# A Conformer block on one core: the list scheduler takes in the head and the first loads, and models the copies as one line

## Chip, cores and metric

The kernel runs on 1 core of one Trainium2 chip. The metric is the device time in microseconds; before the change it is 1916.58 us, the median of 3 runs (1914.57 to 1916.84). The core's engines are named as in the profile: PE (TensorE; PEld are its weight loads), DVE (VectorE), ACT (ScalarE), POOL (GpSimd) and SP (SyncE, which issues nearly all copies). A "copy" below is a DMA transfer.

## The reference

One Conformer block on x of shape 2 x 4000 x 512 in bf16 (B = 2, T = 4000, D = 512, F = 2048, a convolution over 3 tokens):

```python
h = _layernorm(x);  h = _silu(h @ w_ff1_a) @ w_ff1_b
x1 = x + 0.5 * h
h = _layernorm(x1); q, k, v = h @ w_q, h @ w_k, h @ w_v
p = _softmax(einsum('btd,bsd->bts', q, k) * scale)
x2 = x1 + einsum('bts,bsd->btd', p, v) @ w_o
h = _layernorm(x2) @ w_pw1;  h = h[..., :D] * _sigmoid(h[..., D:])
dc = depthwise convolution of h over 3 tokens with dw
dc = (dc - mean over all tokens) / sqrt(variance over all tokens + 1e-05)
x3 = x2 + _silu(dc) @ w_pw2
h = _layernorm(x3); h = _silu(h @ w_ff2_a) @ w_ff2_b
return _layernorm(x3 + 0.5 * h)
```

## The kernel before

**Tiles and stages.** The 8000 tokens are cut into 16 chunks of 4 tiles of 127 tokens (the last chunk of each batch is shorter). The program (`program`, L2515) goes through four stages:

1. The head: x of chunk 0 and the first feed-forward's weights are loaded, chunk 0 is normalised and transposed on TensorE, and its first four blocks are computed (`head`, L1131). It takes the first 12 us.
2. First feed-forward (`ff1`, L2566), chunk by chunk, to about 410 us. Beside it the next chunk's x is loaded (`load_x`, L1013), normalised (`ln_job`, L1064) and transposed by a copy (`transpose`, L980: 128 KB, one for each tile); x1 goes out to a DRAM buffer (`put_x`, xd) and the normalised tokens to another (keysd).
3. Attention, to about 1412 us, one group of queries after the other. Keys are read back from keysd, transposed by copies (`key_queries`, L2178) and combined on VectorE into a form stored in DRAM (kfd); values go the same way (v12d). The groups of attention load both again, 384 KB and 256 KB at a time. The convolution of finished chunks runs beside it; its output is stored (dcvd).
4. From 1412 us: the last convolution, the statistics over all tokens, and the second feed-forward (`ff2`, L2798), with x from xd and the convolution from dcvd (`fetch_conv`, L2365), which ScalarE turns into SiLU values (`swish`, L2433).

A second version of the program, for scores beyond a limit, stands behind a branch and does not run with these inputs.

**What sets the order of the work.** Every instruction is emitted through `Sync`, which adds the semaphore waits that its reads and writes need. Each engine executes its own list in order: an instruction that waits holds up all that stand behind it on that engine. Up to L2539 (loads, constants, head) the order is the order of the program. From `S.planned(16000, 8000)` at L2541 on, instructions are collected as nodes of a `Plan` and emitted at the end in the order that a list scheduler finds (`Plan.run`, L234).

The scheduler runs a model of the five engines six times (`once`, L256) and keeps the order with the earliest end. A node has a duration `dur` on its engine, and a time `land` after its start when its result can be read. Each node also has a due time `late`. For TensorE's nodes it is their start in the pass before; for the others it is counted backwards from the readers (L261). An engine takes, of the nodes that are ready in the model, the one that is due first, unless this would hold up one that is ready soon and due earlier (`choose`, L272). A node may be taken up to 16000 ns of TensorE work ahead of TensorE's oldest open node (L283); TensorE itself may swap work within 8000 ns.

A copy's cost before (`Plan.dma`, L213) depends on its own size alone, in ns and bytes:

```python
dur = 1000 + size / 400 if turn else 450 * len(calls)
land = dur + 2600 if turn else dur + 2000 + size / 200
```

`turn` marks a transposing copy. Copies do not slow each other down in this model. The loads ahead of L2541 are not in the plan at all: for the plan their data is there from the start.

Instructions emitted by the plan all carry line L93 in the profile (the recorded call), so they are told apart by the tiles they write and read: wff are the feed-forward weights and stage buffers in the same place, xt the x tiles and, during attention, the loaded keys and values, keys the hidden activations, keys and convolution data, work the small buffers with normalised tokens, sums the matmul operands made on VectorE, s and y the PSUM banks.

Of the kernel before, what the change touches and what calls it, by code (L numbers as in the profile page):

```python
# [61 lines left out]
class Ev:  # L62
    __slots__ = ("key", "val", "snap")
# [7 lines left out]
class Buf:  # L71
# [3 lines left out]
    __slots__ = ("name", "w", "r", "excl", "alias")  # L75
# [9 lines left out]
class Call:  # L85

    __slots__ = ("name", "args", "kw")
# [16 lines left out]

class Node:

    __slots__ = ("e", "emit", "dur", "land", "preds", "succs", "left", "ready", "late", "at", "seq", "ev")


class Plan:  # L110

    PASSES = 6
    TABLES = {AF.Silu: 1, AF.Exp: 2, AF.Tanh: 2, AF.Sigmoid: 3, AF.Sqrt: 4}
    AFTER = {"PE": 65, "ACT": 45, "DVE": 45, "POOL": 60, "SP": 60}
    OVER = {"PE": 0, "ACT": -100, "DVE": -84, "POOL": -60, "SP": 42}
# [56 lines left out]
    def new(self, e, dur, land, emit, reads, writes, dkeys=()):  # L172
        n = Node()
        n.e, n.dur, n.land, n.emit, n.preds, n.succs, n.seq, n.at = e, dur, land, emit, set(), [], len(self.nodes), len(self.pe)
        self.nodes.append(n)
        n.preds |= self.link(n, reads, writes, dkeys)
        return n

    def op(self, e, fn, reads, writes, inc):
# [3 lines left out]
        if e != "PE":  # L183
            n = self.new(e, dur, dur, [lambda: S.emit_op(e, call, reads, writes, inc)], reads, writes)
            if e == "ACT" and call.name == "activation":
                self.tables(n, self.TABLES.get(call.given("func", 2)))
            return
# [25 lines left out]
    def dma(self, engs, dkey, fns, reads, writes):  # L213
        calls = [fn(Probe()) for fn in fns]
        S = self.S
        size = sum(c.given("out", 0).nbytes() if callable(c.given("out", 0).nbytes) else c.given("out", 0).nbytes for c in calls)
        turn = "transpose" in calls[0].name
        dur = 1000 + size / 400 if turn else 450 * len(calls)
        land = dur + 2600 if turn else dur + 2000 + size / 200
        assert len(set(engs)) == 1  # L220
        n = self.new(engs[0], dur, land, [], reads, writes, (dkey,))

        def emit():
            n.ev = S.emit_dma(engs, dkey, calls, reads, writes)

        n.emit.append(emit)
        return n

    def lag(self, a, b):
# [4 lines left out]
    def run(self):  # L234
# [10 lines left out]
        best = None  # L245
        for _ in range(self.PASSES):
            end, order, starts = self.once()
# [8 lines left out]
    def once(self):  # L256

        pe, T = self.pe, self.T
        for n in reversed(self.nodes):
            if n.e != "PE":  # L260
                n.late = min([s.late - self.lag(n, s) for s in n.succs] + [pe[min(n.at, len(pe) - 1)].late + 40000])  # L261
        free = {e: 0.0 for e in self.AFTER}
        wait = {e: [] for e in self.AFTER}
        for n in self.nodes:
            n.left, n.ready = len(n.preds), 0.0
            if not n.left:
                wait[n.e].append(n)
        head, done, starts = 0, [False] * len(pe), [0.0] * len(pe)
        index = {n: k for k, n in enumerate(pe)}
        order = []  # L270

        def choose(e):  # L272
            if e == "PE":
                best = None
                for n in wait["PE"]:
                    k = index[n]
                    if T[k] - T[head] > self.beside:
                        continue
                    key = (max(free[e], n.ready - (40 if k == head else 0)), k)
                    if best is None or key < best[0]:  # L280
                        best = (key, n)
                return best and (max(free[e], best[1].ready), best[1])
            limit = T[head] + self.ahead  # L283
            found = [n for n in wait[e] if T[n.at] <= limit]
            if not found:
                return None
            now = max(free[e], min(n.ready for n in found))
            can = sorted([n for n in found if n.ready <= now], key=lambda n: (n.late, n.seq))
            soon = [n for n in found if n.ready > now]
            for n in can:  # L290
                end = now + n.dur + self.OVER[e]
                if all(end <= u.ready + 60 or u.late >= end or u.late >= n.late for u in soon):
                    return now, n
            u = min(soon, key=lambda n: n.ready)
            return max(free[e], u.ready), u

        ask = dict.fromkeys(free, True)
        said = {}
        while len(order) < len(self.nodes):
            for e in free:  # L300
                if ask[e]:
                    said[e], ask[e] = choose(e), False
            s, n = min([c for c in said.values() if c], key=lambda c: c[0])
            wait[n.e].remove(n)
            ask[n.e] = True
            free[n.e] = s + n.dur + self.OVER[n.e]
            order.append(n)
            if n.e == "PE":
                k = index[n]
                done[k], starts[k] = True, s  # L310
                if k == head:
                    while head < len(pe) and done[head]:
                        head += 1
                    ask = dict.fromkeys(free, True)
            for u in n.succs:
                lag = self.lag(n, u)
                u.ready = max(u.ready, s if lag is None else s + lag)
                u.left -= 1
                if not u.left:
                    wait[u.e].append(u)  # L320
                    ask[u.e] = True
        return free["PE"], order, starts
# [197 lines left out]
class Conformer:  # L520
# [1994 lines left out]
    def program(self, any_score):  # L2515
        i = self.i
        self.any_score = any_score
        S = self.S
        self.reset_schedule()
        self.out_evs = []  # L2520
        self.ring, self.third, self.fourth = list(range(4)), None, None
        self.place(0, self.slot(0, 5))

# [13 lines left out]

        self.act(self.nr1, self.onef, AF.Silu, [self.b_onef], [self.b_nr1])
        self.head()  # L2539
        if not any_score:  # L2540
            S.planned(16000, 8000)  # L2541

        def weights():
            for n, name in (("q", "w_q"), ("k", "w_k"), ("v", "w_v")):
# [352 lines left out]
```

## Time and profile before

| | |
|---|---|
| median of 3 runs | 1916.58 us |
| the profiled execution | 1912.87 us, with a span of 1909.0 us from first to last instruction |
| mean granted clock of TensorE | 0.995 |
| copies | 231.82 MB, 121 GB/s over the span |
| SyncE's queue | 45.8% of the 16 copy engines' span; ScalarE's queue 0.1% |

The rows that the steps below use of copies, from their issue to their landing (the middle value of each group):

| copy | number, size | us to landing |
|---|---|---|
| work<-work, transposing | 206 | 2.5 |
| keys<-keysd, transposing | 62 | 3.4 |
| xt<-kfd | 98 of 384 KB | 3.2 |
| xt<-v12d | 105 of 256 KB | 2.9 |
| kfd<-xt (store) | 14 of 384 KB | 3.8 |
| keys<-dcvd | 12 of 508 KB | 4.3 |
| wff<-in_w_ff_a_dram | 15 of 256 KB | 5.4 |
| wff<-in_w_ff_b_dram | 8 of 512 KB | 7.3 |

How to read it. In the timeline a line gives the start, the length, the engine, the instruction and its tiles as out<-in, and in brackets how long the engine had been idle before it and what ended that. Merged instructions of one kind share a line, with their number behind an x. The releaser in brackets is inferred: a wait for several semaphores is put down to the one that came last. TensorE's busy time counts from a matmul's start to its modelled end, at whatever clock was granted.

### The profile page before, as it was taken

What the parts mean: (1) busy time and instruction counts of PE and PEld (TensorE: products, weight loads), DVE (VectorE), ACT (ScalarE), POOL (GpSimd) and SP (SyncE); (2) the same over time, 40 slices, a digit from 0 to 9 for tenths busy, and PEclk for the clock granted to TensorE, in tenths of its full rate; (3) what the DMA queues carried; (4) which work ended last, traced back from release to release, by engine and by line L of the source; (5) the groups of instructions that cost most, each with busy time, mean ns of one, the idle gap of its engine ahead of it and who ended that gap; (6) DMA issues with size and microseconds to landing.
All of it is one profiled execution on the core that took longest, in us unless ns stands there. A gap on an engine that the chain in (4) does not pass through costs nothing.

```text
span 1909.0 us, 38976 instructions
## 1 busy us (share of the span) xinstructions
PE 1869.8 (98%) x15359; PEld 1505.4 (79%) x15362; DVE 1574.6 (82%) x3315; ACT 1178.3 (62%) x2061; POOL 132.5 (7%) x235
## 2 busy tenths in 40 slices
PE   8999999999999999999999999999988999999998
PEld 5899999965777777777577777777764899999897
DVE  6789888858788889888888788878976888888875
ACT  4777777644555555566346555655556777777773
POOL 1000000000000000000000000000011000000000
PEclk9999999999999999999999999999999999999999
DMA  7333344297655565457944553454366222312211
GB/s 188 83 84 87 84 113 105 58 273 194 168 139 142 153 184 159 116 130 173 239 125 124 134 124 109 128 139 118 112 192 171 61 61 77 77 46 59 51 42 33
DMA packets 333645, 231.82 MB, mean 121 GB/s; under 512 B 208264, under 2 KB 305867, under 8 KB 333199
## 3 DMA queue, kind: packets, MB, share of 16 engines
q1 hardware_dynamic: 332777, 228.91, 45.8%
q8 instruction: 123, 2.02, 0.4%
q14 instruction: 67, 0.55, 0.1%
q10 hardware_dynamic: 678, 0.34, 0.1%
HBM read 128.30 MB, written 55.65 MB: 96 GB/s over the span
## 4 chain that ended last, share of the span: by engine, by line
PE 90%; DVE 4%; DMA 3%; SPq 2%; issue 1%; ACT 1%; DVEq 0%
PE y L93 46%; PE s L93 44%; SPq L93 2%; DVE work L93 1%; DVE sums L93 1%; DVE s L93 1%; DVE wff L93 1%; DVE xt L93 1%; DMA keys<-dcvd 0%; DMA kfd<-xt 0%; SPq L978 0%; DMA wff<-in_w_ff_b_dram 0%; DMA keys<-keysd 0%; DMA wff<-keysd 0%; DMA work<-work 0%
## 5 line engine op out<-in xcount | busy, mean ns | idle before, releaser
L93 ACT ACTIVATE sums<-s 128x508 bf16<-128x508 f32 (+2 forms) x494 | 289.1, 585 | 281.9 <-PE s L93 281.1
L93 ACT ACTIVATE keys<-s 128x508 bf16<-128x508 f32 (+1 forms) x281 | 163.8, 586 | 189.7 <-PE s L93 165.6
L93 PE MATMUL y<-work,keys 128*127 128x256 bf16 x1920 | 244.7, 273 | 0.0
L93 PE MATMUL s<-work,keys 128*128 128x254 bf16 (+5 forms) x1456 | 228.5, 293 | 2.6 <-DVE xt L93 2.4
L93 DVE TENSOR_TENSOR sums<-sums 128x508 bf16<-128x508 bf16 (+4 forms) x528 | 193.7, 398 | 40.9 <-ACT sums L93 37.5
L93 PEld LDWEIGHTS y<-work,keys 128*127 128x127 bf16 x1920 | 216.3, 137 | 5.2
L93 PE MATMUL y<-wff,keys 128*127 128x256 bf16 (+3 forms) x1592 | 209.2, 276 | 0.1
L93 DVE BATCH_NORM_STATS2 work<-xt 127x6 f32<-127x512 bf16 x307 | 201.7, 681 | 5.9 <-DMA xt<-in_x_dram 4.7
L93 PE MATMUL y<-sums,keys 128*128 128x254 bf16 (+1 forms) x1440 | 202.5, 270 | 0.0
L93 PE MATMUL s<-sums 128*128 128x254 bf16 x1296 | 194.3, 273 | 0.0
L93 DVE TENSOR_TENSOR keys<-keys 128x1016 bf16<-128x1016 bf16 (+2 forms) x262 | 168.1, 660 | 31.0 <-ACT keys L93 23.5
L93 PEld LDWEIGHTS y<-wff,keys 128*127 128x127 bf16 (+1 forms) x1592 | 176.1, 136 | 14.1 <-issue 3.3
L93 PE MATMUL y<-work,wff 128*128 128x254 bf16 (+2 forms) x1116 | 184.0, 292 | 0.0
L93 ACT ACTIVATE work<-xt,work 127x512 bf16<-127x512 bf16 x204 | 162.1, 810 | 12.6 <-DVE work L93 12.6
L93 POOL TENSOR_TENSOR work<-work 127x4 f32<-127x4 f32 (+3 forms) x90 | 89.9, 1000 | 1124.9 <-DVE work L93 1124.7
L93 PEld LDWEIGHTS y<-sums,keys 128*128 128x128 bf16 x1440 | 139.1, 97 | 26.4 <-issue 0.6
L93 PEld LDWEIGHTS s<-work,keys 128*128 128x128 bf16 (+1 forms) x1456 | 119.2, 97 | 51.0 <-issue 3.3
L93 DVE TENSOR_TENSOR work<-work,sums 128x508 f32<-128x508 f32 (+1 forms) x224 | 150.5, 672 | 2.5
L93 PE MATMUL s<-work,wff 128*128 128x508 bf16 (+3 forms) x596 | 138.6, 366 | 5.4 <-ACT keys L93 3.4
L93 PE MATMUL y<-sums,xt 128*128 128x254 bf16 (+1 forms) x960 | 142.4, 270 | 0.3 <-DVE sums L93 0.2
L93 PEld LDWEIGHTS s<-sums 128*128 128x128 bf16 x1296 | 126.7, 98 | 18.1
L93 PE MATMUL s<-work 128*127 128x512 bf16 (+3 forms) x528 | 130.8, 377 | 0.6 <-ACT work L93 0.6
(156 smaller groups left out, 3168.7 us busy)
## 6 DMA issues: line engine op xcount, KB each, us to landing
xt<-kfd SPq DMA_DIRECT2D x98, 384.0 KB, 3.2
xt<-v12d SPq DMA_DIRECT2D x105, 256.0 KB, 2.9
xd<-xt SPq DMA_DIRECT2D x28, 448.0 KB, 2.9
xt<-xd SPq DMA_DIRECT2D x28, 448.0 KB, 4.1
out_dram<-xt SPq DMA_DIRECT2D x14, 448.0 KB, 3.2
dcvd<-wff SPq DMA_DIRECT2D x48, 127.0 KB, 2.1
keys<-dcvd SPq DMA_DIRECT2D x12, 508.0 KB, 4.3
xt<-in_x_dram SPq DMA_DIRECT2D x13, 448.0 KB, 4.1
```

The source lines that it names most:

```text
L93: return getattr(eng, self.name)(*self.args, **self.kw)
```

## The change

The plan starts earlier: `S.planned(16000, 8000)` moves from behind the head to the start of the program, ahead of the first loads. The loads of x and of the first feed-forward's weights, the constants' memsets and the whole head become nodes of the plan. Two of these loads carry issuers of both SyncE and ScalarE; the assertion that a copy has one issuer is dropped, and such a node stands on its first issuer, SyncE.

Copies get a size and pass through one line in the model. A copy begins to move when it is issued and the line is free, moves at 260 bytes a ns (180 for a transposing one), and can be read 1000 ns after its last byte. So a copy behind others lands later in the model. The closed formulas for `dur` and `land` change too; they serve where the line's answer of a pass is not there yet. `choose` counts a copy as taking at least its time on the line. And a copy's due time is 3000 ns earlier than its readers ask (`SPARE`).

```diff
 class Plan:
+    SPARE = 3000
...
-        dur = 1000 + size / 400 if turn else 450 * len(calls)
-        land = dur + 2600 if turn else dur + 2000 + size / 200
-        assert len(set(engs)) == 1
+        dur = 800 + size / 350 if turn else 450 * len(calls)
+        land = 1600 + size / 180 if turn else dur + 1400 + size / 260
...
+        n.size, n.turn = size, turn
...
-                n.late = min([s.late - self.lag(n, s) for s in n.succs] + [pe[min(n.at, len(pe) - 1)].late + 40000])
+                n.late = min([s.late - self.lag(n, s) - (self.SPARE if n.size else 0) for s in n.succs] + [pe[min(n.at, len(pe) - 1)].late + 40000])
...
-        order = []
+        order, pipe = [], 0.0
...
-                end = now + n.dur + self.OVER[e]
+                end = now + max(n.dur, n.size / 260) + self.OVER[e]
...
             order.append(n)
+            if n.size:
+                begin = max(s + (400 if n.turn else n.dur + 400), pipe)
+                pipe = begin + n.size / (180 if n.turn else 260)
+                n.land = pipe - s + 1000
...
     def program(self, any_score):
...
+        if not any_score:
+            S.planned(16000, 8000)
...
         self.head()
-        if not any_score:
-            S.planned(16000, 8000)
```

No instruction's operands, tile or amount of work changes; the order on each engine can.

More of the change, by code (lines that the diff above doesn't have):

```diff
@@ L105 @@
 class Node:
-    __slots__ = ("e", "emit", "dur", "land", "preds", "succs", "left", "ready", "late", "at", "seq", "ev")
+    __slots__ = ("e", "emit", "dur", "land", "preds", "succs", "left", "ready", "late", "at", "seq", "ev", "size", "turn")
 class Plan:
     PASSES = 6
+    SPARE = 3000
     TABLES = {AF.Silu: 1, AF.Exp: 2, AF.Tanh: 2, AF.Sigmoid: 3, AF.Sqrt: 4}
@@ L174, in new @@
         n.e, n.dur, n.land, n.emit, n.preds, n.succs, n.seq, n.at = e, dur, land, emit, set(), [], len(self.nodes), len(self.pe)
+        n.size, n.turn = 0, False
         self.nodes.append(n)
```

## The prediction

> **What bounds the kernel now.** I read the page's busy shares first, then TensorE by stage, then the long idle spells of TensorE, then for each what the engine that ended it had itself been waiting for, and last how full the copy engines were there. On the page:
>
> ```profile
> span 1909.0 us, 38976 instructions
> PE 1869.8 (98%) x15359; PEld 1505.4 (79%) x15362; DVE 1574.6 (82%) x3315; ACT 1178.3 (62%) x2061; POOL 132.5 (7%) x235
> ```
>
> TensorE is busy for 98% of the span, so this change, which alters no arithmetic and no tile, can only win what TensorE idles: 1909.0 - 1869.8 = 39.2 us, some 6 us of it after the last matmul. By stage (window, its length, PE busy and count, granted clock, share of the copy engines, GB/s):
>
> ```profile
> 80.00:400.00 320.00, 320.00 (x2909) 1.00 0.39 99
> 480.00:900.00 420.00, 417.85 (x3470) 1.00 0.58 153
> 960.00:1380.00 420.00, 418.20 (x3437) 1.00 0.45 122
> 1480.00:1900.00 420.00, 419.87 (x3571) 1.00 0.23 56
> ```
>
> Over 1580 us TensorE idles 4.1 us. The rest sits in the head and in three passages between stages: 400 to 480, 900 to 960 and 1380 to 1480. Four spells there are over 2 us. The timeline gives them in brackets, with who ended them; the line ahead of each is the instruction that held up that engine:
>
> ```profile
> 22.21 2.36 DVE L93 TENSOR_TENSOR work<-wff 128x2048 bf16<-128x2048 bf16 x2 [5.15 <-DMA wff<-in_w_ff_b_dram]
> 24.96 1.89 PE L93 MATMUL y<-work 127*128 127x127 bf16 x16 [4.79 <-DVE work L93]
> ...
> 426.58 0.42 DVE L93 TENSOR_TENSOR xt<-keys 128x512 bf16<-128x512 bf16 x1 [3.72 <-DMA kfd<-xt]
> 429.65 0.61 PE L93 MATMUL s<-sums,keys 128*128 128x254 bf16 x4 [3.73 <-DVE sums L93]
> ...
> 938.21 0.43 DVE L93 TENSOR_TENSOR xt<-keys 128x512 bf16<-128x512 bf16 x1 [3.04 <-DMA kfd<-xt]
> 941.75 1.17 PE L93 MATMUL s<-work,keys 128*128 128x508 bf16 x4 [2.45 <-DVE xt L93]
> ...
> 1465.03 1.51 ACT L93 ACTIVATE work<-keys,work 128x508 bf16<-128x508 bf16 x2 [5.62 <-DMA keys<-dcvd]
> 1467.16 3.39 PE L93 MATMUL s<-work,wff 128*128 128x508 bf16 x9 [3.45 <-ACT keys L93]
> ```
>
> All four have one shape. An in-order engine (VectorE three times, ScalarE once) was given an instruction that reads or overwrites what a copy has in hand; the copy landed late; work that TensorE needed, and that was ready, stood behind it. The planner's copy times set that order. Together they are 4.79 + 3.73 + 2.45 + 3.45 = 14.4 us of idling.
>
> Each costs more than its idle time. Around its end the granted clock falls; the stages just behind three of them:
>
> ```profile
> 430.00:434.00 4.00, 4.00 (x16) 0.57 0.89 234
> 434.00:438.00 4.00, 4.00 (x29) 1.00 0.89 262
> 942.00:946.00 4.00, 4.00 (x16) 0.57 0.83 256
> 1468.00:1472.00 4.00, 3.93 (x11) 0.57 0.24 42
> ```
>
> TensorE counts as busy, but at 0.57 of its clock over 4 us, so 0.43 x 4 = 1.7 us is lost each time; behind the first spell, 24.9 to 60 us, the clock is 0.96 over 35.1 us, some 1.4 us. Idle spells up to 1.57 us (at 1393.06) have no such dip. [...]
>
> **The change part by part.** *Copy times.* The last second-layer weight load is issued at 14.64 and lands 7.55 us later (chain of waits). It is issued before planning starts, so the plan of before knows nothing of it and takes its weights as present. For the kfd store issued at 931.46 (393216 bytes) the old formula says 450 + 2000 + 393216/200 = 4.4 us; VectorE got past it at 938.21, 6.75 us later, because two loads of 512 KB went out at 930.32. By the new line, these start at 930.32 + 0.9 + 0.4 = 931.62 and take 1048576/260 = 4.03 us, the store 1.51 us, and 1.0 us more: 938.16. For the dcvd load of 1456.17 (520192 bytes) the old formula says 5.05 us; the chain shows 8.83. By the new line, 4.19 MB of weight loads issued from 1444.14 on take 16.1 us, the x load after them 2.0, the load itself 2.0 and 1.0 more: about 1466, against 1465.0. The 260 fits the full stages (234 to 262 GB/s at shares of 0.83 to 0.89). So the new plan sees three of these four waits to within 1 us, and an engine that picks among ready instructions takes others first. The wait that ends at 426.58 is different: the store was issued at 423.78 and took 2.8 us, under the old 4.4; the queue of SyncE, busy without a pause from 412 to 436, was behind its plan. There the line helps only because it is loaded and puts the reader later.
>
> What is then late next, spell by spell:
> - Head: the norm factor of chunk 1 is ready at 17.14 + 1.02 = 18.16; the four normalisations (1.38 us) need no weights and can end by 19.8. TensorE runs out at 20.17, and three blocks of chunk 0 (12 matmuls, at 26.64 in the trace) cover the transposes. At most 4.79 + 1.4 = 6.2 us goes. VectorE's idle time that can be used is 5.15 us, and it is 82% busy after that (28.73 of 35.10 us), so I take 5.0, with 3 to 6.2 as ends.
> - 429.65: the sums that TensorE awaits take 1.54 us and their last input is there at 424.66 + 0.59 = 425.25, so TensorE could go on at 426.8 instead: 2.8 + 1.7 = 4.5 us.
> - 941.75: TensorE waits for a bank that VectorE empties in 0.74 us; its matmuls end by 937.4. Nothing else is late: 2.45 + 1.7 = 4.2 us.
> - 1467.16: ScalarE stood idle while the block of 1460.10 was ready at about 1461. 3.45 + 1.7 = 5.2 us.
>
> The three make 13.9 us if all go. A new order in crowded passages brings waits of its own, and the first of the three was not a misjudged copy, so I take half: 7.0, with ends 0 and 13.9.
>
> *The head in the plan.* It removes no instruction. What can move: the memsets on VectorE (0.86 to 3.22 us) now come by due time; the weight load on ScalarE's queue can go ahead of the two 15-row pieces of x there and put them back by its issue time, 0.42 us; on SyncE's queue the order x, then weight slices, stays by due time. x 0 is read at 3.25, just as the last memset ends, and TensorE stands 0.87 us at 8.38 for the second weight slice whatever the x tiles do. I count 0, with ends -0.9 and +0.9.
>
> *The reserve of 3 us* (every copy due that much earlier) puts VectorE and ScalarE work that feeds a store ahead of other work, and stores past loads on SyncE's queue. The order among copies changes only where several stand ready; outside the passages SyncE mostly waits for data (245.8 us for TensorE's y, 216.5 for ScalarE's keys). Nothing new is waited for, but an issue that comes earlier than its data holds up all copies behind it. It can win at most TensorE's 2.15 + 1.80 us of idling in the two attention stages; the loss is the rival below. I take 0.
>
> Sum: 5.0 + 7.0 = **12.0 us**. Against the profiled execution, 1912.87 us with a span of 1909.0 and 3.9 us around it, this gives a span of 1897.0. The median of before is 1916.58, 3.7 above the profiled time; the same difference there gives **1904.6 us**.
>
> **Rivals.** (1) *Only the head.* The plan spreads the passages' copies anew and a different instruction stands before a different late copy: 1916.58 - 5.0 = 1911.6. For: SyncE's queue at 412 to 436 is full, and a plan cannot shorten it. Against: the formula meets 938 and 1465.
>
> (2) *Slower, by transposing copies that are now thought faster than they are.* The 206 work<-work copies take 2.5 us in the middle (their landing row). The old formula gives 131072/400 + 3600 ns = 3.93 us, the new one without a queue 0.4 + 0.73 + 1.0 = 2.13, now 0.37 us short. Four make one chunk's input, so some 51 chunks; if TensorE or the engine before it comes to each just on the planned landing, 51 x 0.37 = 19 us comes in, against 12 won: 1924. It decides from the point where the plan's margin before the reader falls under 0.37 us. For: TensorE is full between 80 and 400 us, so any wait counts whole. Against: TensorE idles 0.00 us there, and the reserve asks for these copies earlier.
>
> (3) *It does not do what it says.* SyncE already issues what is ready at once; the new order wins the head and gives it back in new waits in the passages, where one new spell of 2.5 to 3.7 us costs 4 to 5 us with its clock dip: about 1916.
>
> **How the numbers follow.** Forecast 0.53, own range 1895 to 1911; only the head 0.13; slower 0.22; nothing 0.12. A difference of 0.2%, 3.8 us, is about what measuring this kernel can tell from none. Faster is forecast and first rival, 0.66; same 0.12; slower 0.22. The low end takes 6.2 + 13.9 + 0.9 = 21.0 us: 1895.6, so 1895; the high end is the slower rival, 1924.
>
> **What would show it.** The idle spell of 4.79 us before the first transposes of chunk 1 is gone, with VectorE's normalisations ahead of the sums of the second layer's weights; VectorE's and ScalarE's waits for kfd<-xt and keys<-dcvd shrink below 1 us each; the granted clock stays at 1.00 behind the passages; TensorE's busy time hardly changes and the span falls by its idling. I am wrong if spells over 2 us stand at other places, if TensorE idles over 1 us between 80 and 400 or after 1480, or if the stage 480 to 900 loses more than its 2.15 us.

## The result

The changed kernel takes 1892.3 us (median of 4 runs, 1891.78 to 1893.78) against 1916.09 (4 runs, 1914.57 to 1916.84): a ratio of 0.9878, 95% interval 0.9861 to 0.9895, 23.8 us less. The forecast was 12.0 us less, 1904.6, with a range down to 1895. The direction was right and the size half of the measured one; the time lies 2.7 us below the range.

The page of the changed kernel, its span and engines:

```profile
span 1887.7 us, 38980 instructions
PE 1864.2 (99%) x15362; PEld 1503.1 (80%) x15362; DVE 1575.4 (83%) x3315; ACT 1181.0 (63%) x2061; POOL 133.3 (7%) x235
```

The span is 21.3 us shorter. TensorE's idling falls from 39.2 to 1887.7 - 1864.2 = 23.5 us, 15.7 us less; its busy time falls by 5.6 us although it does the same matmuls. The stages (window, length, PE busy and count, granted clock, share of the copy engines, GB/s) show why:

```profile
20.00:55.00 35.00, 35.00 (x227) 1.00 0.59 121
80.00:400.00 320.00, 319.06 (x2889) 1.00 0.42 103
400.00:475.00 75.00, 75.00 (x485) 1.00 0.81 225
890.00:950.00 60.00, 58.76 (x398) 1.00 0.91 221
1370.00:1460.00 90.00, 81.89 (x573) 1.00 0.71 194
```

All four spells over 2 us are gone (the longest idle spell left is 1.49 us), and so are the four dips of the clock: it is 1.00 in every stage shown. VectorE's waits for kfd<-xt (9.6 us in three, the longest 3.7) and ScalarE's for keys<-dcvd (5.6 us in one) have left the list of waits. In before the clock is at half (0.50) for 3.41 us from 24.33, 430.51, 942.51 and 1468.16; that accounts for most of the 5.6 us: about 6.5 us by the prediction's count (1.4 + 3 x 1.7), less some 1.4 us by which the warm-up matmuls of the head take longer now (5.68 us against 4.25).

At the four places, the timeline of the changed kernel (start, length, engine, instruction, and in brackets the idle time before it and what ended it):

```profile
17.48 1.39 DVE L93 TENSOR_SCALAR work<-xt,work 127x512 bf16<-127x512 bf16 x4 [1.20 <-POOL work L93]
20.98 1.06 PE L93 MATMUL y<-work 127*128 127x127 bf16 x16
23.76 2.35 DVE L93 TENSOR_TENSOR work<-wff 128x2048 bf16<-128x2048 bf16 x2
...
419.41 1.55 DVE L93 TENSOR_TENSOR sums<-sums 128x508 bf16<-128x508 bf16 x4 [0.20 <-ACT sums L93]
421.47 0.43 DVE L93 TENSOR_TENSOR xt<-keys 128x512 bf16<-128x512 bf16 x1 [0.51 <-PE y L93]
...
920.20 0.52 SPq L93 DMA_DIRECT2D kfd<-xt  x1
920.76 2.89 SPq L93 DMA_DIRECT2D keys<-vhd  x3
...
1439.38 2.10 SPq L93 DMA_DIRECT2D keys<-dcvd  x3
1444.25 5.12 PE L93 MATMUL s<-work,wff 128*128 128x508 bf16 x23 [1.49 <-DVE work L93]
1445.31 0.59 ACT L93 ACTIVATE keys<-s 128x508 bf16<-128x508 f32 x1 [2.22 <-PE s L93]
```

In the head VectorE normalises chunk 1 (17.48) ahead of the weights' sums (23.76), and the transposes run at 20.98 without a wait. In the first passage the sums for TensorE come ahead of the key work. In the second a kfd store goes out ahead of the last three 512 KB loads (920.20 and 920.76); in before it stood behind the last two. In the third ScalarE takes the block's activations and no longer stands before the dcvd load. In passages 1 and 3 the readers moved; in passage 2 the copies did.

To place the difference I put both traces on one scale: matmuls in order, each worth its columns divided by 2400 (us; a scale of mine, near the traces' pace, where one 508-column matmul follows another after 215 ns, the median of both kernels; one on a quarter of the array, of which four start within 0.01 us at 443.50 in after, counts a quarter), and the time at which each kernel has done the same sum (some 1792 us of work in all). The table gives the difference to the profiled execution of before, in us, by stage of that scale; negative is time won. The row of after adds up to 22.0 us, against 21.3 of the spans: three matmul records are missing in the trace of before, 0.6 us of work.

| kernel | head, to 55 | 55-390 | passage 1, 390-480 | 480-870 | passage 2, 870-930 | 930-1290 | passage 3, 1290-1380 | after it |
|---|---|---|---|---|---|---|---|---|
| after | -6.0 | +1.2 | -7.3 | +0.8 | -2.4 | -0.4 | -7.9 | 0.0 |
| e1 head alone | +0.9 | 0.0 | -0.2 | +1.9 | -1.0 | +1.3 | +0.5 | 0.0 |
| e2 line, no head | -0.6 | 0.0 | -7.1 | +1.4 | -4.2 | -0.4 | -5.9 | +0.2 |
| e3 no reserve | -4.2 | 0.0 | -7.3 | +2.9 | -3.3 | +3.0 | -10.0 | +0.2 |
| e4 no line | +2.5 | +2.8 | -0.4 | +1.5 | +2.3 | -2.2 | +4.5 | 0.0 |
| e9 first weights on SyncE | -7.2 | 0.0 | -7.3 | -1.5 | -3.3 | -1.9 | -8.4 | +0.1 |

### The profile page after: what moved, and what is told of

Same layout as the page of the kernel before. It is cut to its first block, busy times and chain, and to the rows that moved or that the text cites. A ratio compares the mean times of both kernels' runs of the same rounds, so it can differ in the third digit from the quotient of the medians.

```text
span 1887.7 us, 38980 instructions
## 1 busy us (share of the span) xinstructions
PE 1864.2 (99%) x15362; PEld 1503.1 (80%) x15362; DVE 1575.4 (83%) x3315; ACT 1181.0 (63%) x2061; POOL 133.3 (7%) x235
## 4 chain that ended last, share of the span: by engine, by line
PE 93%; DVE 3%; ACT 1%; DMA 1%; issue 0%; SPq 0%; POOL 0%; ACTq 0%; DVEq 0%
PE s L93 47%; PE y L93 46%; DVE work L93 2%; ACT work L93 1%; DMA work<-work 1%; DVE sums L93 1%; DVE xt L93 0%; DVE s L93 0%; DMA wff<-keysd 0%; ACT sums L93 0%; DVE wff L93 0%; SPq L93 0%; DMA xt<-in_x_dram 0%; POOL work L93 0%; ACT xt L93 0%
## 5 line engine op out<-in xcount | busy, mean ns | idle before, releaser
L93 PE MATMUL s<-work,keys 128*128 128x254 bf16 (+5 forms) x1456 | 224.6, 291 | 0.8 <-ACT sums L93 0.6
L93 PE MATMUL s<-work,wff 128*128 128x508 bf16 (+4 forms) x660 | 139.9, 348 | 3.6 <-DVE work L93 2.8
L93 PE MATMUL s<-work 128*127 128x512 bf16 (+2 forms) x541 | 137.0, 383 | 1.8 <-DVE work L93 1.2
```

What stands on the lines that cost most here:

```text
L93: return getattr(eng, self.name)(*self.args, **self.kw)
```

## The experiments

The times are medians; the ratio is to before on the same chip, with its 95% interval. The theory after the result: the line does it, because the plan then knows which copies stand in a queue. Rivals: the reserve, a mere lateness of the planned copies, the choice among copies, and luck (any new order would have got rid of a bad old one).

**e1**: before, with the plan's start ahead of the loads and nothing else.

```diff
+        if not any_score:
+            S.planned(16000, 8000)      (ahead of the first loads, and not behind the head)
-        assert len(set(engs)) == 1
```

> Before, with the plan's start moved ahead of the first loads and nothing else (old copy times, no line, no reserve). Line theory: the head wins the 6.0 us that the trace after shows at TensorE's 55th microsecond of work, the passages at 430, 942 and 1467 us keep their spells: about 1910. Reserve theory: the same, 1910. Luck theory (any new plan throws the passages anew, and the old throw was a bad one): the three spells mostly vanish here too, 1895 to 1903.

1919.89 us, 1.0033 (1.0019 to 1.0047): slower than before. No theory expected the head to lose. Its timeline:

```profile
20.97 1.23 DVE L93 TENSOR_TENSOR work<-wff 128x2048 bf16<-128x2048 bf16 x1 [6.55 <-DMA wff<-in_w_ff_b_dram]
32.81 0.69 DVE L93 BATCH_NORM_STATS2 work<-xt 127x6 f32<-127x512 bf16 x1 [3.99 <-DMA xt<-in_x_dram]
36.53 1.09 PE L93 MATMUL y<-work,keys 128*127 128x256 bf16 x8 [3.06 <-DVE keys L93]
```

Planned with the old copy times, VectorE still meets the weights early (6.55 us of waiting) and then stands 3.99 us before x of chunk 2; TensorE's spell has moved from 24.96 to 36.53. The plan knew of the loads and thought them faster than they are. The three later spells stay (4.08 us at 431.56, 1.85 at 944.63, 2.71 at 1471.54). Luck would have removed some.

**e2**: after, with the plan's start back behind the head.

```diff
-        if not any_score:
-            S.planned(16000, 8000)      (ahead of the first loads)
         self.head()
+        if not any_score:
+            S.planned(16000, 8000)
```

> After, with the plan's start back behind the head. Line theory: the passages' 15 us stay won, the spell of 4.8 us before chunk 1's transposes comes back with its clock dip: 1892 + 6 = 1898. Reserve theory: the same. Luck theory: the passages are thrown anew, anywhere from 1895 to 1912.

1896.73 us, 0.9905 (0.9889 to 0.9922). The spell before chunk 1's transposes is back (4.70 us at 24.89) and the passages stay won: as the line theory expected. With e1: the head in the plan is worth +0.9 us without the line and -5.4 with it (-6.0 against -0.6).

**e3**: after, without the reserve.

```diff
-    SPARE = 3000
+    SPARE = 0
```

> After, with the reserve at 0 instead of 3000 ns. Line theory: the line alone puts the readers of late copies behind ready work, so 1892 within 4 us. Reserve theory: copies go out later again, waits of VectorE and ScalarE for copies return in the passages, 1900 to 1907. Luck theory: 1890 to 1905.

1896.7 us, 0.9909 (0.9893 to 0.9926): the reserve does not carry the win. Its interval still overlaps that of after. e3 loses 5.5 us against after in the two attention stages (2.9 + 3.0 against 0.8 - 0.4), and its list of waits has an entry that no other kernel with a line of 260 has, TensorE itself waiting for a transposing copy (engine, what for: us, times, longest):

```profile
PE s L93 <- DMA work<-work: 5.6, 7, 1.7
```

So the reserve may be what keeps these waits away; one kernel without it does not show it.

**e4**: after, without the line; the change's own closed formulas alone.

```diff
-            if n.size:
-                begin = max(s + (400 if n.turn else n.dur + 400), pipe)
-                pipe = begin + n.size / (180 if n.turn else 260)
-                n.land = pipe - s + 1000
-                end = now + max(n.dur, n.size / 260) + self.OVER[e]
+                end = now + n.dur + self.OVER[e]
```

> After, without the line: a copy lands by the change's own closed formulas, whatever stands before it; head in the plan and reserve kept. Line theory: the plan no longer sees the queues, so spells of 2 to 4 us with clock dips stand at the kfd store and the dcvd load again, 1905 to 1910, and the head's weights are thought early, so part of its 6 us goes too. Reserve theory: issues 3 us ahead cover the queues, 1892 within 4 us. Luck theory: 1890 to 1905.

1924.01 us, 1.0051 (1.0035 to 1.0068): worse than before, and by more than any theory said. The closed formulas suit a copy alone and are shorter than the old ones (3.4 us for the kfd store, against 4.4), so readers come even earlier:

```profile
948.47 0.29 DVE L93 TENSOR_TENSOR sums<-keys 128x256 bf16<-128x256 bf16 x1 [5.32 <-DMA keys<-keysd]
951.32 1.03 PE L93 MATMUL s<-work,keys 128*128 128x508 bf16 x2 [4.81 <-DVE xt L93]
...
1468.75 1.23 DVE L93 TENSOR_TENSOR work<-wff 128x2048 bf16<-128x2048 bf16 x1 [6.41 <-DMA wff<-in_w_ff_b_dram]
1470.91 1.11 PE L93 MATMUL y<-work 127*128 127x127 bf16 x8 [5.92 <-ACT work L93]
```

The reserve is in this kernel and does not help; the reserve theory falls here.

**e5**: e4, with every copy planned 3000 ns later.

```diff
-        land = 1600 + size / 180 if turn else dur + 1400 + size / 260
+        land = 4600 + size / 180 if turn else dur + 4400 + size / 260
```

> After, without the line, but every copy is planned to land 3000 ns later than by the change's closed formulas, alone or behind others. Lateness theory (the line helps only because it makes the plan put readers later): the kfd store is planned at 6.4 us against 6.75 measured, the weights at 6.9 against 7.6, so the spells go as with the line: 1892 to 1896. Line theory (the plan must know which copies stand in a queue): a copy alone, 3.2 us measured for xt<-kfd, is planned at 6.4, and TensorE's and VectorE's order in attention suffers; the long queues are still missed: 1898 to 1908.

1924.7 us, 1.0035 (1.0018 to 1.0051). Lateness alone does not do it, though the long copies are planned to within 1 us, dcvd's excepted: ScalarE waits 6.7 us for that one, VectorE 6.3 us for weights and 4.7 for a v12d store. It is worse than the line theory's own range, too. What e5 rules out is this one constant.

**e6, e7, e10, e11**: after, with another speed of the line (the same two constants and the one in `choose`).

```diff
-                pipe = begin + n.size / (180 if n.turn else 260)
+                pipe = begin + n.size / (360 if n.turn else 520)      (e6; e10: 208, 300; e11: 159, 230; e7: 130, 190)
```

> After, with a line of 520 and 360 bytes a ns in place of 260 and 180. Line theory: the queues in the passages are thought half as long, so the readers of the kfd store and of the dcvd load come 2 to 4 us early: 1898 to 1906. If only the order of the copies matters and not their landing times: 1892 within 4 us.

> After, with a line of 190 and 130 bytes a ns. Line theory: readers are put later than needed; a reader that is put late costs little as long as TensorE has other work, so 1892 to 1897. Lateness theory: the same or better, 1889 to 1893.

> After, with a line of 300 and 208 bytes a ns, 15% faster. With 520 the time was 1926, with 260 it is 1892. If the win needs a line near the 234 to 262 GB/s that the full passages move: 1895 to 1903, since queues of 5 us are missed by 0.7. If the win were a matter of chance between 260 and 520: anywhere from 1890 to 1926.

> After, with a line of 230 and 159 bytes a ns, 12% slower. With 190 the time was 1915, as before the change. If the win needs a line near the measured rate: 1893 to 1903, with spells that the plan itself asks for (TensorE's order changed for copies that in truth have landed). If by chance: anywhere from 1890 to 1915.

| line, bytes a ns | us | ratio to before, interval |
|---|---|---|
| 190 | 1915.26 | 0.9995 (0.9984 to 1.0006) |
| 230 | 1903.2 | 0.9937 (0.9922 to 0.9952) |
| 260 (after) | 1892.3 | 0.9878 (0.9861 to 0.9895) |
| 300 | 1894.58 | 0.9899 (0.9883 to 0.9914) |
| 520 | 1926.39 | 1.0055 (1.0038 to 1.0072) |

The win stands at 260 and 300, at or a little above what the full stages move (234 to 262 GB/s in the prediction's rows), and goes on both sides; e6 came out 20 us over the range expected of it. The two sides lose in different ways, as the lists of waits show. With 520 VectorE waits for copies again: 10.8 us for the second layer's weights, 3.8 for kfd stores, 3.0 for keys. With 190 and 230 no wait of VectorE or ScalarE for these copies or for keys<-dcvd is left, and TensorE waits for VectorE's xt instead, 10.8 us and 6.1 us, against 1.6 in after. With 300 VectorE waits 5.9 us for kfd stores, and passage 1 wins 5.0 us in place of 7.3.

e7 was not expected to lose all of the win: I had thought that a reader put too late costs little. Its like, e11, shows the price in the passage. The first line is the window 445 to 465 of after, the other two e11 (window, length, busy time and count of PE, PEld, DVE, ACT, POOL, clock, copies; then a wait):

```profile
445.00:465.00 20.00, 20.00 (x150) 13.68 (x149) 19.66 (x51) 7.04 (x12) 0.00 (x0) 1.00 0.68 216
```

```profile
445.00:465.00 20.00, 14.10 (x84) 7.72 (x83) 16.82 (x43) 7.55 (x14) 0.00 (x0) 1.00 0.36 118
```

```profile
PE y L93 <- DVE xt L93: 6.1, 2, 4.8
```

The copies run at a third of their engines (0.36) while TensorE idles 5.9 us: it waits for key operands that VectorE makes late. In after VectorE is busy 19.66 of these 20 us, which leaves little room to catch up on work that was put off.

**e8 and e12**: after with more passes, and after with the old count in `choose`.

```diff
-    PASSES = 6
+    PASSES = 14                         (e8)
-                end = now + max(n.dur, n.size / 260) + self.OVER[e]
+                end = now + n.dur + self.OVER[e]      (e12)
```

> After, with 14 passes of the planner in place of 6: the same model, another order. It measures how much one order differs from another under the same knowledge. Line theory: 1892 within 4 us. Luck theory: anywhere from 1885 to 1905.

> After, with the old count of a copy's time in the choice of the next instruction (issue time alone); landing times still come from the line. Line theory: the landing times do the work, so 1892 within 5 us. If it is the choice among copies (a big one held back for an urgent one) that wins: the spells at the kfd store and the dcvd load return, 1900 to 1907.

1895.86 us, 0.9893 (0.9876 to 0.9909), and 1896.32 us, 0.9903 (0.9888 to 0.9919). Both keep the passages (-7.3 and -6.8 us in the first). So the planned landing times carry the win and not the choice among copies, and another order under the same knowledge is worth some 4 us: the luck in these numbers. After is the fastest of the kernels with its head and line; e8, e12 and e13 (below) win 17 to 21 us against their runs of before.

**e9**: after, with the first weight slice on SyncE's queue.

```diff
-                self.load_wa(i["w_ff1_a"], ti // 2, "ACT" if ti == 1 else "SP")
+                self.load_wa(i["w_ff1_a"], ti // 2, "SP")
```

> After, with the first weight slice issued on SyncE's queue in place of ScalarE's. In the trace after, ScalarE's queue issues it ahead of its two small pieces of x, and VectorE waits 2.18 us for x at 5.03 us. If that order costs the 1.0 us by which TensorE is behind at its tenth microsecond of work, the head wins about 1 us more: 1891 with the same luck elsewhere. If the wait is hidden behind the weights anyway, nothing: 1892; another throw in the passages moves either by 4.

1884.56 us (5 runs), 0.9847 (0.9833 to 0.986): faster than both kernels, and some 6 us under the lower of the two expectations. After first, then e9; ScalarE's first issues and VectorE's first read of x:

```profile
0.74 0.45 ACTq L93 DMA_DIRECT2D wff<-in_w_ff_a_dram  x1
5.03 1.29 DVE L93 BATCH_NORM_STATS2 work<-xt 127x6 f32<-127x512 bf16 x2 [2.18 <-DMA xt<-in_x_dram]
```

```profile
0.74 0.67 ACTq L93 DMA_DIRECT2D xt<-in_x_dram  x1
3.01 0.69 DVE L93 BATCH_NORM_STATS2 work<-xt 127x6 f32<-127x512 bf16 x1 [0.16 <-DMA xt<-in_x_dram]
```

The change had let 256 KB of weights ahead of 15 rows of x on ScalarE's queue. Undone, VectorE starts 2.0 us earlier; of that the head keeps 1.2 us (-7.2 against -6.0). The clock is no rival here: in after the 13 warm-up matmuls, all at half speed, end at 6.86 us, and TensorE then stands 0.69 us more for VectorE (7.55), so a quicker start of the clock would not have brought its next matmuls forward. TensorE is 0.8 to 1.0 us behind before at its tenth microsecond of work in after, e8, e12 and e13, whose ScalarE queue issues in the same order. The other 6 us of e9's lead come from the order behind it.

**e13, e14, e15**: after and e9 with transposing copies planned as slow as measured, and e9 with another reserve.

```diff
-                n.land = pipe - s + 1000
+                n.land = pipe - s + (1400 if n.turn else 1000)      (e13 on after, e15 on e9)
-    SPARE = 3000
+    SPARE = 2500                                                    (e14, on e9)
```

> After, with transposing copies planned 400 ns later (1400 ns behind the last byte), which is 2.5 us alone, as measured. If their early planning costs what the slower rival said: VectorE's 15.5 us of waits for work<-work fall under 5 us and the time falls by up to 5 us, 1887 to 1891. If VectorE had the time to wait: 1892 within 4 us, with the waits gone.

> The version with the first weight slice on SyncE's queue, with transposing copies planned 400 ns later. If their early planning costs: 1880 to 1884. If not: 1884 within 4 us, or as far as orders differ, up to 1892.

> The version with the first weight slice on SyncE's queue (1884.6), with a reserve of 2500 ns in place of 3000: another order behind the same head. If that version's lead over the change is its head: 1891 less nothing, 1889 to 1892. If it belongs to the better plan that a true head allows: 1883 to 1887. If orders simply differ by several us: anywhere from 1883 to 1895.

1897.75 us, 0.9916 (0.99 to 0.9933); 1889.99 us, 0.9874 (0.9858 to 0.9891); 1886.65 us, 0.9855 (0.9838 to 0.9871). Planning the transposing copies later wins nothing, and both expectations of e13 were wrong: VectorE's waits for them are 18.0 us in e13 and 16.9 in e15, against 15.5 in after and 16.1 in e9, so the early planning is not what makes these waits; what does stays open. e14 differs from e9 by 2 us. The three kernels with e9's head lie at 1885 to 1890, the four with after's head and a line of 260 (after, e8, e12, e13) at 1892 to 1898. So much of e9's lead goes with its head, but why a head that is 1.2 us faster should order the rest better was not tested.

## Why the prediction was wrong in size

- **What bounds the kernel**: right. The whole win is TensorE's idling (15.7 us) and its busy time (5.6 us), which is the clock dips less the longer warm-up; the prediction had 6.5 for the dips. With the 2.45 us spell the dip behind it went, too: the clock is 0.57 over 942 to 946 us in before and 1.00 over 890 to 950 in after.
- **Head, 5.0 us**: measured 6.0, within its ends. But it was put down to the plan's knowing of the loads. e1 shows that this alone loses 0.9 us; it needs the line's landing times as well. The number came near because the spell was counted rightly; the cause that it was given was incomplete.
- **Three spells, 7.0 us**: this is the term that failed. The prediction worked out 4.5 + 4.2 + 5.2 = 13.9 us and took half. Measured: 7.3 + 2.4 + 7.9 = 17.6, over the 13.9 that it held to be the most. It is no luck of one order: after, e2, e3, e8, e12 and e13, all with a line of 260, win 15.5 to 20.6 us in the three passages together. The halving had two reasons. That the first spell was not a misjudged copy did not matter: readers are put behind ready work all the same, and the passage's smaller spell (0.69 us at 451.85) goes with it. That a crowded passage breeds new waits did not hold while the line's speed was the true one: passage 1 wins 7.1 to 7.3 us in after, e2, e3, e8, e9 and e13, and 6.8 in e12, whatever the order. Passage 2 gave 2.4, less than its 4.2. In passage 3 the idle spells of 1.57 us at 1393 and 1.47 at 1430 became shorter as well (0.49 at 1378.75 and 0.52 at 1415.82); that was not in the sum.
- **The head's order of issues, 0 with 0.9 either way**: TensorE is 1.0 us behind at its tenth microsecond of work; e9 gives 1.2 back. That TensorE stands "for the second weight slice whatever the x tiles do" was wrong: x came late enough to be what it stood for (0.69 us at 7.55, for VectorE).
- **The reserve, 0**: e3 lies 4 us over after, as much as one order differs from another. The stages between the passages give back 1.6 us in after (+1.2, +0.8, -0.4), which the prediction left to the rival.
- **The rivals.** Of the slower one, the waits came and hardly any of the price: VectorE waits 15.5 us in 19 waits for work<-work, 3.9 in 3 before (11.0 and 4.5 below), and TensorE idles 0.94 us between 80 and 400.

```profile
DVE sums L93 <- DMA work<-work: 11.0, 14, 1.7
DVE work L93 <- DMA work<-work: 4.5, 5, 1.4
```

Mostly VectorE had the time. Once it had not: the copy issued at 282.38 landed 3.44 us later, VectorE waited the 1.69 us for it that stand as the longest above, and TensorE stood the 0.94 us, at 288.75, for what VectorE made next. That is the better part of the +1.2 us between 55 and 390. "Only the head" and "it does not do what it says" are refuted by e2 and by the table.

- **From the profile to the median**: the prediction worked with one profiled execution of before (1912.87 us) and added 3.7 us to come to its median. That execution was a quick one: of 38 others of before, on four chips, only three were quicker, and they ran from 1910.72 to 1920.71 us. After, the profiled time is 0.5 us under the median (1891.78 and 1892.3). So the profiles differ by 21.1 us, just about the 21.0 of the range's low end, and the medians by 23.8. With 3.7 us added, the profile of after would have given 1895.5 us, inside the range; the added term, taken from one execution, is what put the time outside it. It was the halved term that left the forecast at 12.0.

## What to carry to other kernels

Where a scheduler orders in-order engines, a copy's landing time has to count what stands before it in the queue, at the rate that the trace's full stages move: a rate 12% under it cost 11 us here, 27% under it 23 us and twice the rate 34 us, while 15% over it cost no more than one order differs from another. Adding one constant (3 us) to all copies did not help, and adding more of the program to the plan with wrong copy times made it slower. A short idle spell of TensorE should be priced with the clock dip that the trace shows behind it, 1.4 to 1.7 us here for spells of 2.45 to 4.79 us. And look at what a planner does to the first few issues by hand: one load ahead of a small one on a second queue cost the head 1.2 us here.

## What the runs showed of the hardware

The dip is not tied to the length of one spell alone. In after, idle spells of 1.01, 0.46 and 1.49 us follow each other from 1439.88 on without a dip: the first 18 matmuls of 508 columns from 1444.25 on take 4.04 us. In e2 the same three instructions stand behind spells of 1.02, 0.46 and 1.49 us from 1443.55 on and have one: the first 12 such matmuls from 1447.91 on take 4.37 us there. A spell of 1.57 us followed by one of 0.41 has no dip in before (1393.06; the clock is 1.00 from 1390 to 1400). The spell of 1.85 us in e1 (944.63) has none: the four 508-column matmuls behind it take 1.03 us, as four take 1.02 at 946.39. What decides between a dip and none is not shown. In the head the 13 warm-up matmuls, of 508 columns, start at 1.19 us in before and at 1.18 in after. In after all of them follow each other after 400 to 425 ns, half speed against the 215 ns at full clock; in before they do so up to 3.70 us, and from 3.99 on it is 214 or 215 ns. Full clock is on record from 3.85 us in before and from 6.97 in after. The 13 take 4.25 us in the one and 5.68 in the other.
